# Attention beside a gated-Strassen feed-forward layer: first products taken apart, x reloads put back, `wo` in the q and k buffers

## The chip, the cores and the metric

The kernel runs on one core of a Trainium2 chip. The metric is device time in microseconds (us). Of the kernel before, three runs took 1152.2, 1151.22 and 1151.04 us; the median is 1151.22 us. The engines are TensorE (PE, with PEld for its weight loads), VectorE (DVE), ScalarE (ACT), GpSimd (POOL) and SyncE (SP); an engine executes its own queue in order and waits on semaphores for others. SP and POOL issue nearly all DMAs here.

## What is computed

x has 2048 rows of 576 numbers, all in fp32. It is normalised, and two branches of the result are added to x:

```python
def _A_ref(x, wqkv, wo):            # 32 heads of 18
    q, k, v = split(x @ wqkv)
    idx = pos[:, None] - arange(8) * 2          # 8 keys, every second position back
    logits = einsum("bhsd,bhswd->bhsw", q, k[idx]) * scale   # masked where idx < 0
    return einsum("bhsw,bhswd->bhsd", softmax(logits), v[idx]) @ wo

def _B_ref(x, w1, w2):              # 576 -> 4608 -> 576
    return maximum(x @ w1, 0) @ w2

xn = _layernorm(x)
return x + _A_ref(xn, wqkv, wo) + _B_ref(xn, w1, w2)
```

## The kernel before

The rows are taken in two phases (`ph`) of 1024 rows, each held as eight tiles `X[i]` of 128 rows. In a phase the 4608 columns of w1 come in 18 blocks `n` of 256; m = 18 ph + n counts them. Each block has two halves of 512 rows, and g = 2m + h numbers these 72 steps. Every fp32 product is made of parts: a number is cast to a high and a low part (`hi_lo`, L287: ACT makes the high part, DVE the low one), and PE multiplies high by high, high by low and low by high.

The products with w1 are made from step 4 on by a scheme of seven products instead of eight (`pstep`, L627: P1, P5, P6, P2, P7, P3, P4). It needs sums and differences of x (`xs`, forms S1 to S4, from `s_forms`, L379) and of w1 (a set of eight slots, `wset`, from `set_make`, L446: DMAs from a copy kept in DRAM, four DVE differences in `ts`, four casts of 512). Its results go through the PSUM banks `bk` and `bkA` and the SBUF sums `sn` to `hhi` and `hlo`. Between these steps the outputs of the step before are made: `o_step` (L743) multiplies h with w2 into `po`. `po` is seeded with x by ACT (`po<-x`) and copied back to x (`x<-po`). In the last block of a phase the row is stored (L783), and in phase 0 POOL then reloads it with the raw x of phase 1 (L785), for the seeds of phase 1.

Attention goes in four units `u` of eight heads per phase. Block `QP[ph][u]` projects q, k and v (`qkv_tile`, L802) into `qo`, `kk` and `v`; `halo` (L840) copies the seven neighbouring positions over by DMA (L843). Then DVE does the attention (L848): products and sums for the logits (L870, L873), softmax, products with v (L902), and eight transposes into a `pr` buffer (L916), which four DMAs write to DRAM in turned order (L923). There are two `pr` buffers. At block `WOP[ph][u]` `wo_make` (L541) loads the rows of wo and casts them; `wo_h` (L689) loads the turned output (`olo<-turned`, L704 and L708) and casts it to `ohi` and `olo`; `o_step` adds their products into `po`. u = 4 there stands for the 16 left-over columns per unit.

Near the end of phase 0, the second phase's x is prepared: `x_load` (L1035) fetches a tile into a `pr` buffer, `x_norm` (L1040) normalises it (the power for `rstd` is a POOL instruction, L321; the last step on DVE is L335), `x_raw` and `x_rest` (L1043, L1051) transpose it on PE through the bank `pm`, and ACT copies it to `kk`, `v` and `qo`, which are free for it at that time; `x_parts` and `x_done` make the parts.

The order of every queue is written out in advance by a planner (class `Order`, L54). A dictionary `plan` gives functions to (step, tick) places; one tick passes after each of the seven P products and each `o_step`. `send` and `keep` issue a DMA at that point on SP or POOL. `act` and `dve` put an operation with a due time into a list, and `pick` (L81) gives out, among the operations that are ready by the planner's clock, the one that is due first:

```python
                if best is None or op.due < best[0].due:
                    best = (op, now)
```

`later` puts attention's DVE work into a queue that is served when nothing else is ready. When a PE product or a DMA needs an operation that is not out yet, `force` gives it out first. All that is planned time; on the chip only the queues' order and the semaphores remain.

## Time and profile before

| | us |
|---|---|
| median of three runs | 1151.22 |
| the profiled execution | 1153.78 |
| its span, first to last instruction | 1152.0 |
| PE busy | 1126.6 |
| DVE busy | 822.0 |
| ACT busy | 754.0 |
| POOL busy | 201.3 |

The profile comes from one execution, and all its times count from the start of its span. Busy time is the time in which an engine worked on instructions; the registers' and DMA-issuing instructions are not in it. A wait is put down to the instruction whose semaphore came last. The granted clock (PEclk) is TensorE's clock as a share of full speed. DMA issues stand under SPq and POOL. In rows of instructions the columns are start, duration, engine, line, operation, output and inputs, the count, and in brackets the idle time ahead of it with what ended it.

### The profile page before, as it was taken

The page shows a single profiled execution, that of the slowest core. Times are in us where ns is not written, and L with a number is a line of the kernel's source. Part 1 is how long each engine was busy: PE and PEld are TensorE (multiplying, and loading weights), DVE is VectorE, ACT ScalarE, POOL GpSimd, SP SyncE. Part 2 cuts the span into 40 slices and gives each one's busy share as a digit, 9 for nine tenths or more (in the row PEclk, how much of TensorE's full clock was granted, in tenths as well). Part 3 has the DMA queues.
Part 4 walks back from the last instruction along what each step waited for, and adds up shares of the span by engine and source line. Part 5 has one row for each costly group of instructions (what it writes and reads, how often), then busy time and mean ns, then how long its engine had stood idle before and what let it go on. Part 6 is the DMA issues. An engine that isn't in the chain of part 4 may idle for free.

```text
span 1152.0 us, 22365 instructions
## 1 busy us (share of the span) xinstructions
PE 1126.6 (98%) x8528; PEld 1111.0 (96%) x8528; DVE 822.0 (71%) x1533; ACT 754.0 (65%) x1658; POOL 201.3 (17%) x408
## 2 busy tenths in 40 slices
PE   7999999999999999999989999999999999999998
PEld 6899999999999999999989999999999999999998
DVE  7649979872999179964783398688936995399831
ACT  5558457754777477676686577387737765577764
POOL 2323322531436122620120001000000000000000
PEclk9999999999999999999999999999999999999999
DMA  5254263553444344264362222231323222322322
GB/s 164 62 172 137 77 172 97 160 133 103 137 142 130 72 136 122 70 145 149 96 182 65 82 60 65 46 103 53 94 46 94 68 56 62 98 59 58 82 70 92
DMA packets 137788, 115.64 MB, mean 100 GB/s; under 512 B 56288, under 2 KB 115936, under 8 KB 136400
## 3 DMA queue, kind: packets, MB, share of 16 engines
q1 hardware_dynamic: 128192, 85.00, 26.8%
q0 software_dynamic: 9344, 28.91, 8.8%
q8 instruction: 67, 1.10, 0.4%
q14 instruction: 41, 0.34, 0.1%
q10 hardware_dynamic: 144, 0.29, 0.1%
HBM read 96.01 MB, written 36.50 MB: 115 GB/s over the span
## 4 chain that ended last, share of the span: by engine, by line
PE 87%; DVE 4%; DMA 3%; ACT 3%; issue 1%; SPq 1%; POOL 0%; ACTq 0%; DVEq 0%; POOLq 0%
PE po L285 40%; PE bk L285 27%; PE pm L285 15%; PE bkA L285 6%; DMA x<-in_x 1%; DVE wset L282 1%; ACT po L279 1%; ACT x L279 1%; ACT wset L279 1%; DMA turned<-pr 1%; DMA wset<-wqc 0%; DVE hlo L577 0%; DMA qo<-in_w 0%; SPq L551 0%; DVE ts L282 0%
## 5 line engine op out<-in xcount | busy, mean ns | idle before, releaser
L285 PE MATMUL po<-w2t,hhi 128*128 128x256 f32 (+1 forms) x2304 | 396.6, 294 | 2.1 <-ACT po L279 2.0
L285 PEld LDWEIGHTS po<-w2t,hhi 128*128 128x128 f32 x2304 | 335.1, 188 | 4.1 <-ACT po L279 3.1
L279 ACT ACTIVATE x<-po 128x576 f32<-128x576 f32 x286 | 186.2, 651 | 177.3 <-PE po L285 173.9
L285 PE MATMUL po<-w2t,hlo 128*128 128x256 f32 (+1 forms) x1152 | 244.3, 293 | 0.4 <-DVE hlo L577 0.4
L285 PE MATMUL bk<-xs,wset 128*128 128x256 f32 x1632 | 231.9, 278 | 2.1 <-DVE hlo L577 2.0
L285 PEld LDWEIGHTS bk<-xs,wset 128*128 128x128 f32 x1632 | 211.4, 188 | 3.5 <-DVE hlo L577 2.9
L285 PEld LDWEIGHTS po<-w2t,hlo 128*128 128x128 f32 x1152 | 190.3, 188 | 0.7 <-DVE hlo L577 0.7
L279 ACT ACTIVATE po<-x 128x576 f32<-128x576 f32 x286 | 186.9, 654 | 5.9 <-DVE x L282 0.2
L285 PE MATMUL pm<-wset,xa 128*128 128x432 f32 x768 | 171.4, 360 | 0.8 <-DVE wset L282 0.4
L285 PEld LDWEIGHTS pm<-wset,xa 128*128 128x128 f32 x768 | 140.4, 188 | 7.8 <-ACT qo L279 1.0
L285 PE MATMUL bk<-xa,wset 128*128 128x256 f32 x924 | 132.2, 281 | 4.0 <-DVE sn L282 2.4
L282 DVE TENSOR_TENSOR sn<-bk,sn 128x256 f32<-128x256 f32 x136 | 57.2, 421 | 103.7 <-PE bk L285 63.8
L411 POOL COPY spare<-hhi 1x1 f32<-1x1 f32 x176 | 78.1, 444 | 291.4 <-ACT hhi L279 291.4
L285 PEld LDWEIGHTS bk<-xa,wset 128*128 128x128 f32 x924 | 120.7, 191 | 4.8 <-DVE sn L282 2.8
L279 ACT ACTIVATE kk<-pm 128x144 f32<-128x144 f32 (+1 forms) x68 | 21.0, 308 | 120.2 <-PE pm L285 118.5
L282 DVE TENSOR_TENSOR w2t<-w2t 128x576 fp32r<-128x576 f32 (+1 forms) x72 | 54.1, 751 | 60.8 <-ACT w2t L279 60.2
L870 DVE TENSOR_TENSOR pr<-qo,kk 128x1152 f32<-128x1152 f32 x64 | 84.9, 1351 | 5.6 <-DMA turned<-pr 5.6
L902 DVE TENSOR_TENSOR pr<-lg,v 128x1152 f32<-128x1152 f32 x64 | 85.2, 1356 | 0.0
L873 DVE TENSOR_REDUCE lg<-pr 128x64 f32<-128x1152 f32 x64 | 83.7, 1345 | 0.0
L285 PE MATMUL bk<-xr,wset 128*128 128x256 f32 x426 | 83.5, 278 | 0.0
L279 ACT ACTIVATE hhi<-sn 128x256 fp32r<-128x256 f32 x136 | 56.0, 413 | 35.1 <-DVE sn L282 33.9
L282 DVE TENSOR_TENSOR wset<-wset 128x512 fp32r<-128x512 f32 (+2 forms) x120 | 71.7, 599 | 8.9 <-ACT wset L279 8.5
(133 smaller groups left out, 1484.8 us busy)
## 6 DMA issues: line engine op xcount, KB each, us to landing
w2t<-w2c SPq DMA_DIRECT2D x70, 288.0 KB, 3.0
wset<-w1c SPq DMA_DIRECT2D x106, 128.0 KB, 2.6
w1c<-in_w POOLq DMA_DIRECT2D x72, 144.0 KB, 2.7
w2c<-in_w POOLq DMA_DIRECT2D x72, 144.0 KB, 3.1
wset<-wqc SPq DMA_DIRECT2D x28, 216.0 KB, 2.6
out<-x SPq DMA_DIRECT2D x16, 288.0 KB, 2.1
wset<-w1c SPq DMA_DIRECT2D x70, 64.0 KB, 2.3
ts<-w1c SPq DMA_DIRECT2D x34, 128.0 KB, 2.8
```

Of the source, the lines that this page charges most:

```text
L279: nc.scalar.activation(o, i, func)
L282: nc.vector.tensor_tensor(o, a, b, op=op)
L285: nc.tensor.matmul(o, l, r, start=start, stop=stop, skip_group_check=True)
L411: nc.gpsimd.tensor_copy(spare[0:1], f32(LATEST[-1])[0:1, 0:1])
L870: nc.vector.tensor_tensor(pr[i], q, window(k, i), op=ALU.mult)
L873: nc.vector.tensor_reduce(s["lg"][:, i], pr.pop(i).rearrange(heads, d=Dh), axis=AX.X, op=ALU.add)
L902: nc.vector.tensor_tensor(pr[i].rearrange(heads, d=Dh), e, window(v, i).rearrange(heads, d=Dh), op=ALU.mult)
```

## The change

- Attention's products: the first two products for the logits and their sums ran as product, product, sum, sum. Now the first goes with its sum, then the second; for the planner the first waits for the halo alone and the second for the DMAs of the preceding unit's turned output (`OUT_`).
- Phase 1's raw x: the reload is not issued with the store of the row but four ticks later (`reloads`, `x_again`).
- `wo`: its rows for u = 0 to 3 go to the buffer of q of that unit (`qop`, now two pools of one buffer), not to a `v` buffer; the load waits for that unit's turned output. u = 0 moves one block earlier in both phases (`WOP`). A `v` buffer is given out only when its last readers are (`v_turn`).
- Due times: casts of sets 9 to 12 us instead of 6 to 9, of w2 12 instead of 7, of wo 10 instead of 8; the casts of S3 and S1 4.0 instead of 2.4, those of S2 and S4 9.0 instead of 4.0. P5, P6 and P3 wait each for the form that they read.
- Turned output: for the left-over, the load for the second half's first rows goes out at tick 21 of its step instead of tick 0 of the next. The last but one step's second load goes to a `pr` buffer (`SPARE`) at tick 5 of the last step.
- The set of block 19 is made at tick 6 of step 36, `x_rest` of the last tile moves from tick 13 to 14, `x_done` of the second half from tick 0 to tick 2.

The names `qo`, `rr` and `RD` point to buffers that are now taken from the pools at their use.

```diff
--- before.py
+++ after.py
@@ -26,7 +26,7 @@
 QP = ((0, 3, 7, 11), (1, 4, 8, 12))
-WOP = ((6, 9, 13, 16), (7, 10, 14, 17))
+WOP = ((5, 9, 13, 16), (6, 10, 14, 17))
 HALO = ((0, 112), (112, 127))
@@ -208,6 +208,7 @@
     w2p = pool("w2p", 4)
+    qop = [pool(f"qop{b}", 1) for b in range(2)]
     pad2 = pool("pad2", 1).tile([P, PADS[2]], F32, name="pad2")
...
@@ -249,7 +249,15 @@
-    def v_tile():
+    VLAST = [[], []]
+
+    def v_turn(last):
+
+        o_.force(VLAST.pop(0))
+        VLAST.append(last)
+
+    def v_tile(last=None):
+        v_turn([] if last is None else last)
         return vp.tile([P, 2176], F32, name="v")[:, 0 : (W - 1 + NI) * UD].rearrange("p (w c) -> p w c", w=W - 1 + NI)
@@ -265,8 +273,10 @@
     KR = [raw_view(KK), raw_view(KK)]
-    rr = [z.rearrange("p i c -> p (i c)")[:, 0 : 2 * TBN].rearrange("p (j c) -> p j c", j=2) for z in QO]
-    RD = [rr[0][:, 0], rr[1][:, 0]]
+    QO, rr, RD = [None, None], [None, None], [None, None]
+
+    def q_raw(b):
+        return qop[b].tile([P, NI * UD], F32, name=f"qo{b}")
@@ -385,13 +395,13 @@
         ok = []
-        for j, sl in ((1, 2.4), (0, 4.0)):
+        for j, sl in ((1, 4.0), (0, 9.0)):
             k = act(lambda j=j: copy(XS[h][:, 0, 2 * j : 2 * j + 2], KR[h][j]), 1024, [a4], slack + sl)
         ok += [r, dve(lambda: sub(XR[h][DR:P, 2], RD[h][0:DR], f32(XR[h][0:DR, 2])), TBN, [r], slack + 3.5)]
-        XOK[h, "s"] = ok
+        XOK[h, 10 + S1], XOK[h, 10 + S2], XOK[h, 10 + S4] = ok[0:2], ok[2:4], ok[4:6]
         return ok
@@ -500,10 +510,10 @@
         else:
-            parts(T1, T3, 4, TS[:, 0:2], [c1, c3], 6)
-            parts(T2, T4, 4, TS[:, 2:4], [c2, c4], 7)
-            parts(B11, B21, 2, z[:, B11 : B21 + 1 : 2], [got[B11], got[B21], c1, c4], 8)
-            parts(B22, RR, 2, z[:, B22 : RR + 1 : 2], [got[B22], got[RR], c2, c3], 9)
+            parts(T1, T3, 4, TS[:, 0:2], [c1, c3], 9)
+            parts(T2, T4, 4, TS[:, 2:4], [c2, c4], 10)
+            parts(B11, B21, 2, z[:, B11 : B21 + 1 : 2], [got[B11], got[B21], c1, c4], 11)
+            parts(B22, RR, 2, z[:, B22 : RR + 1 : 2], [got[B22], got[RR], c2, c3], 12)
         ts_free[0] = [*ok[T1], *ok[T3], *ok[T2], *ok[T4]]
@@ -513,7 +523,7 @@
         g = send(lambda: nc.sync.dma_start(f32(w[:, 1]), W2C[m % NP][f * P : (f + 1) * P]), 295, kept["w2", m % NP], 4.0)
-        W2OK[m, f] = hi_lo(w[:, 0], w[:, 1], f32(w[:, 1]), D, [g], 7 + 2 * f)
+        W2OK[m, f] = hi_lo(w[:, 0], w[:, 1], f32(w[:, 1]), D, [g], 12 + 2 * f)
@@ -539,11 +549,15 @@
     def wo_make(ph, u):
-        WO[ph, u] = w = vp.tile([P, 2, D], F32R, name="v")
+        if u < NU:
+            WO[ph, u] = w = qop[u % 2].tile([P, 2, D], F32R, name=f"qo{u % 2}")
+        else:
+            v_turn([])
+            WO[ph, u] = w = vp.tile([P, 2, D], F32R, name="v")
         z = f32(w)[:, 1]
         if u < NU:
-            got.append(send(lambda: nc.sync.dma_start(z, WOC[u * UD : u * UD + P, :]), 295, kept["wo",], 3.0))
+            got.append(send(lambda: nc.sync.dma_start(z, WOC[u * UD : u * UD + P, :]), 295, [*kept["wo",], *turned[ph, u], *OFREE[u % 2]], 3.0))
         else:
@@ -551,7 +565,7 @@
                     ))
-        WOOK[ph, u] = hi_lo(w[:, 0], w[:, 1], z, D, got, 8)
+        WOOK[ph, u] = hi_lo(w[:, 0], w[:, 1], z, D, got, 10)
@@ -636,14 +650,14 @@
-            t = pe(f, T8, [*ok[T1], *ok[RR], *XOK[h, "s"], *XOK[h, 1], *BANK[n3]])
+            t = pe(f, T8, [*ok[T1], *ok[RR], *XOK[h, 10 + S1], *XOK[h, 1], *BANK[n3]])
             BANK[n3] = [act(lambda: copy(SN5, b3), TBN, [t, *SNF[5]], 3)]
         elif name == "P6":
-            t = pe(lambda: terms(b2, slot(m, T2), sform(h, S2), False), T6, [*ok[T2], *BANK[n2]])
+            t = pe(lambda: terms(b2, slot(m, T2), sform(h, S2), False), T6, [*ok[T2], *XOK[h, 10 + S2], *BANK[n2]])
             BANK[n2] = [act(lambda: copy(SN2, b2), TBN, [t, *SNF[2]], 1.4)]
@@ -663,7 +677,7 @@
-            t = pe(f, T8, [*ok[B22], *BANK[n3]])
+            t = pe(f, T8, [*ok[B22], *XOK[h, 10 + S4], *BANK[n3]])
             a = dve(lambda: sub(SN2, b3, SN2, ALU.add), TBN, [t], 0.8)
...
@@ -697,7 +712,13 @@
             ni = 2
-            hi, lo = whp.tile([P, TBN], F32R, name="ohi"), whp.tile([P, TBN], F32R, name="olo")
+            if g == NG - 2 and j == 1:
+                if u < NU:
+                    SPARE[:] = [prp.tile([P, W * UD], F32R, name="pr")]
+                z = SPARE[0][:, 32 + 512 * (u == NU) :]
+                hi, lo = z[:, 0:TBN], z[:, TBN : 2 * TBN]
+            else:
+                hi, lo = whp.tile([P, TBN], F32R, name="ohi"), whp.tile([P, TBN], F32R, name="olo")
             WOH[g, u, j] = hi, lo
@@ -738,6 +759,16 @@
     XLAST = [None] * NI
+    reloads = []
+
+    def x_again():
+
+        for z in reloads:
+            z[0] -= 1
+        while reloads and reloads[0][0] <= 0:
+            _, i, s = reloads.pop(0)
+            XLAST[i] = o_.keep(lambda: nc.gpsimd.dma_start(X[i], x_v[1, i]), 295, s.end)
+
     POF = [[], []]
@@ -778,11 +809,13 @@
             i2 = 4 * G[after[0]][2] + 2 * after[1] + k
+            assert ph == 0 or XLAST[i2] is not None
             POF[k] = [act(lambda: copy(whole(k), X[i2]), D, [e, XLAST[i2]], 2.2)]
             if ph + 1 < NPH:
-                XLAST[i] = o_.keep(lambda: nc.gpsimd.dma_start(X[i], x_v[ph + 1, i]), 295, s.end)
+                XLAST[i] = None
+                reloads.append([4, i, s])
@@ -795,7 +828,8 @@
-    HALOOK = {}
+    HALOOK, VDONE = {}, {}
+    OUT_ = []
     KFREE = [[]]
@@ -803,7 +837,8 @@
             o_.force(KFREE[0])
-            VV[u % 2] = v_tile()
+            QO[u % 2] = q_raw(u % 2).rearrange("p (i c) -> p i c", i=NI)
+            VV[u % 2] = v_tile(VDONE.setdefault((ph, u), []))
             nc.gpsimd.memset(KK[0:1, 0 : W - 1, :], 0.0)
@@ -932,7 +967,7 @@
             OFREE[u % 2] = [send(lambda: nc.sync.dma_start(O16[:, :, 16 * u : 16 * u + 16], qo[:, :, P:UD]), 65)]
-            turned[ph, u] = blocks(OT[u], s["tr"], 4)
+            turned[ph, u] = OUT_[:] = blocks(OT[u], s["tr"], 4)
             if u == NU - 1:
@@ -946,12 +981,13 @@
         add = o_.later
-        first = True
+        done = [[] for _ in range(NI)]
+        done[0], done[1] = halo, OUT_
         for i in range(0, NI, 2):
-            for f in (qk_mul, qk_sum):
-                for j in (i, i + 1):
-                    z = add(lambda f=f, j=j: f(j), big, halo if first else (), 1.3 if f is qk_sum and j == NI - 1 else 0.0)
-                    first = False
+            pairs = [(f, j) for f in (qk_mul, qk_sum) for j in (i, i + 1)]
+            for f, j in pairs if i else [pairs[0], pairs[2], pairs[1], pairs[3]]:
+                after = done[j] if f is qk_mul else ()
+                z = add(lambda f=f, j=j: f(j), big, after, 1.3 if f is qk_sum and j == NI - 1 else 0.0)
         KFREE[0] = [z]
@@ -961,10 +997,11 @@
             for j in (i, i + 1):
-                add(lambda j=j: av_mul(j), big)
+                z = add(lambda j=j: av_mul(j), big)
             for w in (4, 2, 1):
                     add(lambda j=j, w=w: av_add(j, w), w * UD)
+        VDONE[ph, u].append(z)
         for i in range(NI):
@@ -981,7 +1018,9 @@
         p = m - 1
-        if p % NP in QP[p // NP]:
+        if m == NP + 1:
+            at(g, 6, set_make, m)
+        elif p % NP in QP[p // NP]:
             at(g + 1, 0, set_early, m)
@@ -1024,11 +1063,11 @@
                     else:
-                        when = (gg + 1, 0), (gg + 1, 12)
+                        when = (gg, 21) if h else (gg + 1, 0), (gg + 1, 12)
                     if gg == NG - 1:
                     for j in range(len(when)):
-                        at(*when[j], wo_h, gg, z, j)
+                        at(*((gg + 1, 5) if (gg, j) == (NG - 2, 1) else when[j]), wo_h, gg, z, j)
@@ -1078,6 +1117,8 @@
         KR[h] = raw_view(v_tile() if h else KK)
+        rr[h] = q_raw(h)[:, 0 : 2 * TBN].rearrange("p (j c) -> p j c", j=2)
+        RD[h] = rr[h][:, 0]
@@ -1088,7 +1129,7 @@
             ((34, 13), (34, 15), (34, 19), (34, 20)), ((34, 20), (34, 22), (35, 1), (35, 2)),
-            ((35, 3), (35, 5), (35, 9), (35, 11)), ((35, 7), (35, 13)),
+            ((35, 3), (35, 5), (35, 9), (35, 11)), ((35, 7), (35, 14)),
         )
@@ -1098,7 +1139,7 @@
         at(g, 0, x_parts, h, 0)
-        at(g, 0, x_done, h)
+        at(g, 2 * h, x_done, h)
@@ -1110,6 +1151,7 @@
         idx_now[1] += 1
+        x_again()
...
@@ -1249,8 +1291,6 @@
                 o(q, cnt[name])
-        if g == 4:
-            RD[:] = [rr[0][:, 0], rr[1][:, 0]]
     o_.finish()
```

More of the change, by code (lines that the diff above doesn't have):

```diff
@@ L241, in tile_body @@
     VV = {}
-    QO = [keep.tile([P, NI, UD], F32, name=f"qo{b}") for b in range(2)]
     SN5 = keep.tile([P, TBN], F32, name="sn5")
@@ L684, in tile_body @@
     WOH, WOHOK = {}, {}
+    SPARE = []
     OT = dram.tile([NU, NI, P, P], F32, name="turned")
@@ L1134, in tile_body @@
     x_first(3)
-    ST2 = QO[0].rearrange("p i c -> p (i c)").rearrange("p (f d) -> p f d", f=2)
+    ST2 = q_raw(0).rearrange("p (f d) -> p f d", f=2)
     for f in range(2):
@@ L1149, in tile_body @@
     KR[1] = [
-        QO[1].rearrange("p i c -> p (i c)")[:, 0 : 4 * TBN].rearrange("p (s k c) -> p s k c", s=2, k=2),
+        q_raw(1)[:, 0 : 4 * TBN].rearrange("p (s k c) -> p s k c", s=2, k=2),
         TS.rearrange("p s k c -> p (s k c)").rearrange("p (s k c) -> p s k c", s=2, k=2),
```

## The prediction

> **What bounds the kernel.** I read the page's busy times first, then TensorE's (PE) busy time in stretches of the span, then the list of what PE waited for. The page:
>
> ```profile
> PE 1126.6 (98%) x8528; PEld 1111.0 (96%) x8528; DVE 822.0 (71%) x1533; ACT 754.0 (65%) x1658; POOL 201.3 (17%) x408
> ```
>
> PE is busy for 1126.6 of the span's 1152.0 us, and the changed program issues as many products of the same shapes. So the other engines count only where PE stops for them, and at most 25.4 us are there to win. These are the stretches in which it stops; the columns are the length, PE's busy time with its instructions, the granted clock, the DMA share and GB/s:
>
> ```profile
> core 0 of [0], span 1152.0 us
> core 0: us, PE busy (x), PEclk, DMA share, GB/s
> 171.00:184.00 13.00, 9.86 (x75) 1.00 0.43 124
> 184.00:248.00 64.00, 63.11 (x505) 1.00 0.47 136
> 529.00:566.00 37.00, 34.30 (x267) 1.00 0.34 107
> 581.00:588.00 7.00, 3.60 (x18) 0.76 0.37 109
> 584.00:586.00 2.00, 2.00 (x10) 0.50 0.36 139
> 600.00:608.00 8.00, 6.37 (x47) 1.00 0.76 260
> 608.00:1131.00 523.00, 523.00 (x3998) 1.00 0.26 70
> 1131.00:1137.00 6.00, 4.73 (x36) 1.00 0.13 49
> ```
>
> Length less busy time is PE's idle time: 3.14, 0.89, 2.70, 3.40, 1.63 and 1.27 us, together 13.03 us. From 608 to 1131 us it is nil, although the same loops run there. The rest of the 25.4 us lies before 66 us, where the order hardly changes, and behind the last product. The waits after 66 us, with their sum, number and longest:
>
> ```profile
> PE bk L285 <- DVE sn L282: 2.4, 2, 1.3
> PE pm L346 <- DVE pr L335: 2.1, 1, 2.1
> PE po L285 <- ACT po L279: 2.0, 3, 0.9
> PE bk L285 <- DVE hlo L577: 2.0, 4, 0.7
> PE po L285 <- DVE ohi L282: 1.4, 1, 1.4
> PE pm L1054 <- ACT v L279: 1.3, 1, 1.3
> PE po L285 <- ACT ohi L279: 1.3, 1, 1.3
> PE po L285 <- DVE hlo L577: 0.4, 1, 0.4
> ```
>
> These come to 12.9 us: single events of 0.2 to 2.1 us, each with a cause of its own. The question is which of them each edit takes away, and whether the new order makes others.
>
> **The change, part by part.** *First products taken apart (171 to 184 us, 3.14 us).* Attention 1's first two products ran on VectorE (DVE) like this:
>
> ```profile
> 161.32 1.35 DVE L870 TENSOR_TENSOR pr<-qo,kk 128x1152 f32<-128x1152 f32 x1
> 168.28 1.36 DVE L870 TENSOR_TENSOR pr<-qo,kk 128x1152 f32<-128x1152 f32 x1 [5.61 <-DMA turned<-pr]
> ```
>
> The second needs the `pr` buffer that holds attention 0's turned output until its four DMAs have landed. For 5.61 us DVE stands there, and the additions into `sn` behind it, for which PE waits 2.4 us, stand too. SyncE's queue (SP) shows why the DMAs were late:
>
> ```profile
> 154.71 1.46 SPq L843 DMA_DIRECT2D kk<-kk  x2
> 156.28 1.55 SPq L843 DMA_DIRECT2D v<-v  x2
> 157.93 0.88 SPq L934 DMA_DIRECT2D o<-qo  x1
> 158.91 4.13 SPq L923 DMA_DIRECT2D turned<-pr  x4
> ```
>
> In the changed order the last two rows go first and the halo (`kk`, `v`) behind them, and on DVE the first product follows two more pieces of the gated phase (the addition into `sn` and two `hlo`), with its sum and another addition before the second product. With the rows' issue times, starting at 154.71 us, `turned` is out by 159.8 and the `kk` halo by 161.2 us. The halo's landing has this range (minimum, median, maximum):
>
> ```profile
> DMA to landing us min/median/max: 3.3/4.6/6.6
> ```
>
> So the halo is there by 164.5 to 167.8 us. The addition ahead of the first product waits for this group of PE:
>
> ```profile
> 166.61 0.84 PE L285 MATMUL bk<-xs,wset 128*128 128x256 f32 x6
> ```
>
> It ends at 167.45 us, and with the addition and two `hlo` the first product's turn comes after 168 us, when its halo has landed. I take the whole 3.14 us as won; bounds 0 (the halo comes late instead) and 3.14.
>
> *`wo` in the q buffers, u=0 one pair of column blocks earlier (184 to 248 us, 0.89 us).* The products, their casts and one weight load of 288 KB move from n=6 to n=5, and from 7 to 6 in phase 1; count and size stay. The `wqc` loads for the next attention then have no `wo` beside them. The loads wait for attention's DMA too, but that has landed long before (above). I take 0.4 us; bounds -1.0 (a stall like the longest `hlo` wait, 0.7 us, more than once) and 0.89.
>
> The casts for `wo` are the tightest spot of the steady part. In block n=13:
>
> ```profile
> 451.63 0.42 DVE L282 TENSOR_TENSOR olo<-olo,ohi 128x256 fp32r<-128x256 f32 x1
> ```
> ```profile
> 452.56 0.69 PE L285 MATMUL po<-v,ohi 128*128 128x256 f32 x4
> ```
>
> The cast ends 0.51 us before PE asks. The changed order puts this cast and that of the weights ahead of the last of the four set casts, where they stood behind all four, so the margin grows at most of the eight places. At n=5 the cast of `olo` still follows three set casts while attention 1 runs; I charge 0.5 us for it, with 0 and 2.0 us (four `olo` at the margin just read) as ends.
>
> *Due times (529 to 566 us, 2.70 us).* Set casts get due times 3 us later, w2 5 us, `wo` 2 us. The planner always takes the earliest due among the ready operations, so copies in and out of `po` overtake them. That is aimed at the waits of `po` for ACT (2.0 us, three of them, two here and one at 602 us). The second item here is the 1.4 us wait for `ohi`; its load was queued behind a set's loads:
>
> ```profile
> 547.88 1.11 SPq L458 DMA_DIRECT2D wset<-w1c  x2
> 549.03 1.10 SPq L471 DMA_DIRECT2D wset<-w1c  x2
> 550.18 1.98 SPq L708 DMA_DIRECT2D olo<-turned  x2
> ```
>
> The last row is now issued at the end of the step before, ahead of the set's loads and of their wait for PE, at least 2.3 us sooner (550.18 against 547.88). What it passes is delayed by two issues (1.3 us for a set that is wanted 18 us later, below). I take 2.3 of 2.70 us; bounds 0.9 (half of the `ohi` wait and no more) and 2.7.
>
> *x loads behind other work (581 to 588 us, 3.40 us and the clock).* GpSimd's queue:
>
> ```profile
> 576.36 0.61 POOL L785 DMA_DIRECT2D x<-in_x  x1 [5.33 <-ACT v L279]
> 576.98 0.56 POOL L321 TENSOR_TENSOR rstd<-mv,mhalf 128x1 f32<-128x1 f32 x1
> 581.33 0.59 POOL L785 DMA_DIRECT2D x<-in_x  x1 [3.79 <-ACT v L279]
> 581.94 0.57 POOL L321 TENSOR_TENSOR rstd<-mv,mhalf 128x1 f32<-128x1 f32 x1
> ```
>
> Each reload of an x row waits until the old row has been written out, and a `rstd` sits behind it. DVE's last normalisation starts after the second `rstd`, which ends at 582.5 us, and PE's turning had waited 2.1 us when it was done, so PE arrived near 581 us; the `v` copies that follow cost the 1.3 us at L1054. In the changed order the seventh `rstd` is ahead of all reloads and the eighth behind the first reload only, which is free at 576.4 us; then it waits for its own statistics alone, and an estimate from the two holds (the seventh runs at once, the second reload's 3.79 us are gone) puts it 3 to 4 us sooner, ahead of PE. The remainder turnings also move behind P4. In the same place the clock fell to 0.50: 0.76 on average over 7 us is 1.7 us lost, part of it idle; I count 1.3. The reloads themselves go out four ticks later; their rows are wanted only when the next phase's outputs are seeded, a step of the loop later, which covers that (without the cover each would cost up to those four ticks). I take 3.2 + 1.3 = 4.5; bounds 1.3 (only the L1054 wait) and 5.1.
>
> The Trainium skill, TensorE: Matmul & The Clock Gate, Part 1, says that the array falls back to half rate after an idle window of about 3.4 us. The trace does not agree in size, since the pause here is 2.1 us and the row shows 0.50 behind it; by the rule the pause would not be the cause, the clock would stay as it is, and the sum would be 1.3 us smaller.
>
> *Second phase's set later, S forms split (600 to 608 us, 1.63 us).* The casts of block NP+1 leave the stretch in which the last forms of x are made (its loads go out six ticks later), and P5 waits for S1 only. I take 1.2; bounds 0 and 1.63.
>
> *Turned output of the last blocks (1131 to 1137 us, 1.27 us).* The last loads no longer wait for a rotating buffer but go into a free `pr` tile before the preceding `out` stores. I take 1.2; bounds 0 and 1.27.
>
> **The sum.** 3.14 + 0.4 - 0.5 + 2.3 + 4.5 + 1.2 + 1.2 = 12.2 us. The profiled execution took 1153.78 us for a span of 1152.0, so it would become 1141.6. It lies 2.6 us above the median of the three runs, 1151.22 us; on that scale the forecast is 1139.0 us.
>
> **The rivals.** *The halo is late instead.* It now queues behind `turned`. If it lands 3 us after its usual range, DVE stands from 168.6 to 171 us and PE stops about as before: 3.14 us are not won, 1142.1 us. For it speaks that both share SP; against it the 6.6 us maximum.
>
> The Trainium skill, DMA: Bandwidth & Descriptors, Queues, rings and completion order, states that a DMA's completion lands only after earlier writes of the same DMA engine. No row here isolates it; by it this rival's chance rises.
>
> *The phase change stays DVE bound.* If x's forms, not `rstd`, set the pace, PE arrives sooner and waits for `xs` instead: of 4.5 + 1.2 only 1.5 us remain, 1143.2 us. DVE (the third busy time here) is nearly full behind the gap, which speaks for it:
>
> ```profile
> 588.00:600.00 12.00, 11.97 (x99) 11.97 (x100) 10.41 (x21) 10.59 (x21) 1.61 (x3) 1.00 0.71 194
> ```
>
> The four set casts that leave (0.69 us each, a row below) speak against.
>
> *Later casts hurt everywhere.* This one ends slower. The mechanism is a run of four set casts that, with its due time 3 us later, falls in front of a copy that PE waits for, at 34 blocks. Its price is the mean `po` wait, 2.0/3 = 0.67 us: 23 us less the 12.2 gives 1162 us. It decides from 0.36 us a block. Against it:
>
> ```profile
> 528.89 0.69 DVE L282 TENSOR_TENSOR wset<-wset 128x512 fp32r<-128x512 f32 x1
> ```
> ```profile
> 547.68 0.73 PE L285 MATMUL bk<-xa,wset 128*128 128x256 f32 x5
> ```
>
> The set's last cast ends 18 us before the block's P1, so 3 us are there, and the due times give way to the copies, not the reverse.
>
> *The waits only move.* Every gap returns elsewhere: 1151 us.
>
> **How the numbers follow.** The likeliest case, all parts in their bounds near the values taken, has 0.68 and 1136 to 1142 us by itself. The halo rival 0.09, the phase change 0.09, waits that move 0.05, slower 0.09. The largest win is all 13.03 us and the whole 1.7 us of clock, 1136.5; I go a little lower, 1135.3, for the slower first matmuls after each pause that would vanish. The upper end, 1146.5, holds both partial rivals together. Measurement cannot tell less than 0.2% (2.3 us) from no change; faster by more is 0.86, within it 0.05, slower 0.09.
>
> **What would show it.** After: no DVE wait on `turned` and PE's idle time around 171 us gone; no `rstd` behind a waiting reload, clock 1.00 throughout the phase change; `olo` issued before the set at n=16; no wait at 1131 us; PE busy near 1126 us in a span near 1139 us. The prediction is wrong if a new PE wait above 1 us stands at n=5 (about 205 to 235 us), if the first product waits for `kk<-kk`, or if short `po` or `hlo` waits show in the stretch after 608 us.

## The result and the profile after

The changed kernel takes 1137.05 us (median of four runs, 1135.61 to 1137.25) against 1151.13 us before in the same comparison (1150.14 to 1152.2): a ratio of 0.9875, with a 95% interval of 0.9858 to 0.9892. The forecast was 1139.0 us in 1135.3 to 1146.5. The profiled execution took 1137.1 us for a span of 1135.3 us, where before it was 1153.78 us for 1152.0.

The page of the changed kernel, its busy times:

```profile
PE 1120.7 (99%) x8528; PEld 1108.8 (98%) x8528; DVE 825.2 (73%) x1533; ACT 753.3 (66%) x1658; POOL 196.2 (17%) x408
```

PE's idle time went from 25.4 to 14.6 us, and its busy time fell by 5.9 us, although it issues the same 8528 products. Its waits after 66 us, with sum, number and longest, are three instead of the eight kinds of before:

```profile
PE bk L295 <- DVE hlo L591: 1.2, 1, 1.2
PE po L295 <- ACT po L289: 0.3, 1, 0.3
PE bk L295 <- ACT sn L289: 0.2, 1, 0.2
```

PE in stretches (length, busy time with instructions, granted clock, DMA share, GB/s):

```profile
171.00:184.00 13.00, 13.00 (x109) 1.00 0.46 134
529.00:566.00 37.00, 37.00 (x302) 1.00 0.38 118
581.00:588.00 7.00, 6.84 (x56) 1.00 0.81 222
588.00:600.00 12.00, 10.81 (x88) 1.00 0.69 226
608.00:1110.00 502.00, 502.00 (x3837) 1.00 0.26 69
```

All the stretches that stopped are full but for 1.2 us at 590 us and 0.2 us ahead of it, and the clock of 0.50 in the phase change is gone. SP's queue at attention 1, then DVE's, then POOL's at the phase change:

```profile
157.20 3.07 SPq L958 DMA_DIRECT2D turned<-pr  x4
160.37 2.05 SPq L878 DMA_DIRECT2D kk<-kk  x2
```
```profile
170.34 1.35 DVE L905 TENSOR_TENSOR pr<-qo,kk 128x1152 f32<-128x1152 f32 x1
171.61 0.42 DVE L292 TENSOR_TENSOR sn<-bk,sn 128x256 f32<-128x256 f32 x1
...
173.53 1.35 DVE L905 TENSOR_TENSOR pr<-qo,kk 128x1152 f32<-128x1152 f32 x1
```
```profile
566.07 0.55 POOL L331 TENSOR_TENSOR rstd<-mv,mhalf 128x1 f32<-128x1 f32 x1 [3.98 <-DVE mv L328]
567.43 0.67 POOL L770 DMA_DIRECT2D x<-in_x  x1 [0.81 <-ACT v L289]
569.04 0.87 POOL L331 TENSOR_TENSOR rstd<-mv,mhalf 128x1 f32<-128x1 f32 x1 [0.94 <-DVE mv L328]
```

`turned` goes out ahead of the halo, neither product waits, and both `rstd` wait only for their statistics (`mv`), as the prediction said.

**Where the time came from.** The k-th product of PE is the same work at the borders used here, so its start in the kernel before less its start in another trace tells how far the other is ahead. The table gives what is won (+) or lost (-) in each stretch, in us, with the stretches counted on the kernel before's own time. The last column is the sum without the first 66 us: there the traces differ by up to 2.3 us, although all the kernels begin alike, so the first column is left out of what follows.

| kernel | to 66 | to 165 | to 184 | to 290 | to 529 | to 567 | to 590 | to 612 | to end | from 66 on |
|---|---|---|---|---|---|---|---|---|---|---|
| the changed kernel | -1.3 | -0.2 | +4.2 | +1.5 | +1.2 | +3.6 | +5.1 | +0.6 | +2.1 | 18.0 |
| e1 old products | -0.1 | -0.1 | +4.2 | +1.6 | +1.2 | +3.6 | +4.9 | +0.4 | +2.1 | 18.0 |
| e2 reload at once | -1.2 | -0.2 | +4.2 | +1.6 | +1.2 | +3.5 | +1.1 | +0.3 | +2.1 | 13.8 |
| e3 old due times | -1.3 | -0.4 | +4.2 | +1.0 | +0.8 | +2.9 | +4.4 | -1.3 | +1.5 | 13.1 |
| e4 old turned steps | 0.0 | -0.1 | +4.2 | +1.4 | +1.2 | +1.7 | +5.1 | +0.6 | +0.4 | 14.5 |
| e13 old due times and products | -2.2 | 0.0 | +1.5 | +1.0 | -0.9 | +2.7 | +4.4 | -1.3 | +0.8 | 8.2 |
| e5b wo in v | -1.4 | -0.1 | +4.2 | +1.3 | +1.2 | +3.7 | +5.1 | +0.6 | +2.1 | 18.0 |
| e5c no wo edits | -0.7 | -0.1 | +4.2 | -8.9 | +1.2 | +3.5 | +5.1 | +0.6 | +2.0 | 7.6 |
| e10 set early | -0.6 | -0.1 | +4.2 | +1.6 | +1.2 | +3.7 | +4.9 | -0.7 | +2.0 | 16.8 |
| before + new products (e14) | -0.1 | 0.0 | +4.2 | +1.0 | -5.5 | 0.0 | 0.0 | -0.2 | 0.0 | -0.5 |
| before + new due times (e6) | -2.3 | -0.2 | +4.2 | -8.0 | +1.2 | +1.6 | +1.2 | -1.2 | +0.4 | -0.8 |
| e15: e6, planner told of v | -2.2 | -0.2 | +4.2 | -7.6 | +1.2 | +1.7 | +1.1 | -0.8 | +0.3 | -0.1 |

The changed kernel's row tells where. The others tell why, and there the prediction's picture of separate stalls, each with its own edit, does not hold.

### The profile page after: what moved, and what is told of

It is laid out like the page before. It is cut to its first block, busy times and chain, and to the rows that moved or that the text cites. A ratio compares the mean times of both kernels' runs of the same rounds, so it can differ in the third digit from the quotient of the medians.

```text
span 1135.3 us, 22346 instructions
## 1 busy us (share of the span) xinstructions
PE 1120.7 (99%) x8528; PEld 1108.8 (98%) x8528; DVE 825.2 (73%) x1533; ACT 753.3 (66%) x1658; POOL 196.2 (17%) x408
## 4 chain that ended last, share of the span: by engine, by line
PE 96%; ACT 1%; DVE 1%; issue 1%; DMA 0%; POOL 0%; ACTq 0%; DVEq 0%
PE po L295 44%; PE bk L295 30%; PE pm L295 15%; PE bkA L295 6%; ACT x L289 0%; DMA x<-in_x 0%; PE pm L356 0%; DVE wset L292 0%; DVE bst L321 0%; ACT po L289 0%; DVE xa L292 0%; ACT xs L289 0%; ACT xa L289 0%; PE bk L356 0%; DVE x L292 0%
## 5 line engine op out<-in xcount | busy, mean ns | idle before, releaser
L421 POOL COPY spare<-hhi 1x1 f32<-1x1 f32 x176 | 71.6, 407 | 291.5 <-ACT hhi L289 291.5
L911 POOL TENSOR_SCALAR_AFFINE_SELECT lg<-lg 1x512 f32<-1x512 f32 x8 | 10.0, 1246 | 438.0 <-DVE lg L908 438.0
```

The source lines that it names most:

```text
L421: nc.gpsimd.tensor_copy(spare[0:1], f32(LATEST[-1])[0:1, 0:1])
L911: nc.gpsimd.affine_select(out=z, in_=z, pattern=[[1, NI], [1, W], [0, HG]], compare_op=ALU.is_ge, fill=-1e9 / scale, base=1 - W, channel_m ...
```

## The experiments

The theory at the start: the gain is a sum of separate stalls, each taken away by one edit. The rivals: the due times do nearly all; or edits cover for each other. In the table and in each experiment the time is a median of four runs, or of ten for e13, e14, e6 and e15. e13, e14, e6 and e5b ran on a chip where the kernel before scattered from 1150.48 to 1161.76 us. Run beside the experiments, the kernel before had medians of 1152.55 us (e1 to e4), 1153.42 us (those four) and 1152.43 us (the rest), 1.3 to 2.3 us above its 1151.13 us in the comparison above. So 2 us between a median here and 1137.05 us are no evidence by themselves, and the stretches are the better measure.

**The first products in their old order (e1).**

```diff
-            for f, j in pairs if i else [pairs[0], pairs[2], pairs[1], pairs[3]]:
+            for f, j in pairs:
-        done[0], done[1] = halo, OUT_
+        done[0] = halo
```

> The changed kernel with attention's first two products and sums in the old order, and without the dependence on the turned output. Separate stalls (my theory): the second product stands 3 to 6 us for the DMAs of turned again, PE's idle time in 171 to 184 us is 2.5 to 3.2 us again, and with the slower restarts the kernel takes 2.7 to 4.2 us more than the changed one (1139.7 to 1141.3 us). Rival, the stall goes because turned is now issued ahead of the halo and not because of the products: the wait is under 1.5 us and the time stays within 1 us of 1137.05. Rival, the due times do nearly all: within 1 us as well, but with the wait of 3 us still in DVE's row and PE not waiting for it.

Measured: 1136.72 us (1135.87 to 1137.72), and no stall. The edit I had credited with 3.14 us brings nothing in this place. DVE's queue in e1:

```profile
168.95 1.35 DVE L905 TENSOR_TENSOR pr<-qo,kk 128x1152 f32<-128x1152 f32 x1
170.22 0.42 DVE L292 TENSOR_TENSOR sn<-bk,sn 128x256 f32<-128x256 f32 x1
170.56 1.35 DVE L905 TENSOR_TENSOR pr<-qo,kk 128x1152 f32<-128x1152 f32 x1
```

The second product has no wait, because `turned` still goes out ahead of the halo. Something else moved that.

**The old due times (e3).**

```diff
-            parts(T1, T3, 4, TS[:, 0:2], [c1, c3], 9)
+            parts(T1, T3, 4, TS[:, 0:2], [c1, c3], 6)
...
-        W2OK[m, f] = hi_lo(w[:, 0], w[:, 1], f32(w[:, 1]), D, [g], 12 + 2 * f)
+        W2OK[m, f] = hi_lo(w[:, 0], w[:, 1], f32(w[:, 1]), D, [g], 7 + 2 * f)
...
-        WOOK[ph, u] = hi_lo(w[:, 0], w[:, 1], z, D, got, 10)
+        WOOK[ph, u] = hi_lo(w[:, 0], w[:, 1], z, D, got, 8)
```

> The changed kernel with the old due times of the set casts (6 to 9), w2 (7) and wo (8). My theory: PE's waits of po for ACT, 2.0 us in all, and short hlo waits return at 450 to 610 us, and the kernel takes 1 to 3.5 us more (1138 to 1140.6 us). Rival, the due times are what brought most of the whole gain, the order around all other places following from them: 8 us or more (over 1145 us). Rival, the later casts cost time elsewhere: the kernel takes less than 1136 us.

Measured: 1141.79 us (1140.63 to 1142.66), 4.7 us more: above my figure, well below the rival's. PE's two longest kinds of wait in e3:

```profile
PE bk L295 <- DVE hlo L591: 2.4, 2, 2.0
PE po L295 <- ACT po L289: 0.9, 1, 0.9
```

The `po` wait is back as expected; the larger part is an `hlo` wait of 2.0 us at 592 us, in the phase change, and the clock behind it (below). And SP's queue has the halo first again:

```profile
156.47 1.48 SPq L878 DMA_DIRECT2D kk<-kk  x2
...
160.67 4.31 SPq L958 DMA_DIRECT2D turned<-pr  x4
```

So it is the due times that put `turned` first: with the set casts due later, attention 0 is given out sooner. Yet 171 to 184 us stays full in e3, where a sum now stands between the two products. DVE's queue in e3, the first sum and the second product:

```profile
164.47 1.35 DVE L908 TENSOR_REDUCE lg<-pr 128x64 f32<-128x1152 f32 x1
165.86 1.36 DVE L905 TENSOR_TENSOR pr<-qo,kk 128x1152 f32<-128x1152 f32 x1
```

The second product starts 0.9 us after the last `turned` issue has ended (164.98 us), though these DMAs took 3.8 us or more from issue to landing here. So it does not wait for them. The sum has freed the `pr` buffer of the first product, and in the built programs of e3 and e14 the second product has that address, where in the kernel before and in e13 it has the one that `turned` still reads. Either edit should be enough, each in its own way: the due times send `turned` off sooner, and the new order of products does without its buffer.

**Both undone (e13).** The diffs of e1 and e3 together.

> The changed kernel with both the old due times and the old order of attention's first products. Either edit undone by itself left 171 to 184 us without a stall: with the old products, turned was still issued ahead of the halo; with the old due times, the halo was first again but a sum stood between the products. Theory (two covers, each enough): here both are gone, the second product waits 4 to 6 us for turned, PE stops for 2.5 to 3.2 us in that stretch, and the kernel takes 3 to 4.5 us more than with the old due times alone (1141.8 us), so 1144.8 to 1146.3. Rival (a third edit, the wo casts or the v buffers, took the stall away): within 1 us of 1141.8.

Measured: 1148.82 us (1144.04 to 1151.47; span of the profile 1146.0). The stall is back; DVE in e13:

```profile
163.53 1.35 DVE L905 TENSOR_TENSOR pr<-qo,kk 128x1152 f32<-128x1152 f32 x1
168.99 1.36 DVE L905 TENSOR_TENSOR pr<-qo,kk 128x1152 f32<-128x1152 f32 x1 [4.12 <-DMA turned<-pr]
```

PE's idle time there is 1.9 us, less than I expected; the stretch wins 1.5 instead of 4.2 us. That confirms the two covers. The median is above the range I gave, and 1.7 us of it lie between 290 and 529 us, which I did not foresee.

**Each alone on the kernel before (e14, e6).** e14 puts only the new order of products and the dependence on `turned` into the kernel before (the lines of e1's diff, the other way round); e6 only the new due times (those of e3's diff, likewise).

> The kernel before with the new order of the first products and the dependence on turned, and nothing else. Theory: the stall at 171 to 184 us goes as it did with the old due times, PE is idle less than 0.7 us there, and the kernel is 2.5 to 4.5 us faster than before; all other waits (po 2.0, ohi 1.4, pr 2.1, v 1.3, ohi 1.3) stay. Rival (without the other edits the stall stays): same time as before within 1 us.

> The kernel before with the new due times of the set casts, w2 and wo, and nothing else. Theory: the due times alone put turned ahead of the halo, so the stall at 171 to 184 us goes too (3 to 4.2 us), and with it the po waits and the slow stretch at 450 to 483 us (2 to 3 us): 5 to 7.5 us faster than before; ohi at n=16, the rstd and L1054 waits at the phase change and the 1.3 us at the end stay. Rival (due times do nearly all): 10 us or more faster. Rival (they bring only the po waits): 1 to 3 us.

Measured: e14 1153.59 us (1148.25 to 1158.88; ratio 0.9992, interval 0.9962 to 1.0021), e6 1154.7 us (1154.01 to 1156.96; ratio 0.9995, interval 0.9971 to 1.0019). Neither is faster, and both expectations failed, though in both traces the stall at 171 to 184 us is gone with its full 4.2 us. In the profiled executions new stalls take it back. In e6, PE's wait, ACT's row and DVE's last products with v:

```profile
PE pm L285 <- ACT qo L279: 6.3, 1, 6.3
```
```profile
252.90 0.29 ACT L279 ACTIVATE v<-pm 128x144 f32<-128x144 f32 x1 [7.09 <-DVE pr L902]
```
```profile
250.25 2.62 DVE L902 TENSOR_TENSOR pr<-lg,v 128x1152 f32<-128x1152 f32 x2
```

Unit 2's first copy into `v` waits until attention 1 has made its last product with `v`: the two share a buffer. In the kernel before that wait was there too, and hidden, with nothing to spare:

```profile
249.25 0.29 ACT L279 ACTIVATE v<-pm 128x144 f32<-128x144 f32 x1 [0.45 <-DVE pr L902]
```

What used up that margin shows when PE's last products for the first tile of unit 2 are set beside DVE's last product with `v`. In the kernel before:

```profile
247.91 0.56 PE L285 MATMUL pm<-wset,xr 128*128 128x432 f32 x2
```
```profile
247.86 1.36 DVE L902 TENSOR_TENSOR pr<-lg,v 128x1152 f32<-128x1152 f32 x1
```

DVE ends 1.3 us behind that start of PE. In e6 PE starts there at 244.93 us and DVE ends at 252.87, 7.9 us behind. In e14, where PE has won the same 4.2 us, it is 1.0 us (242.78 and 243.74 us), and the copy follows at once, at 243.78 us. So PE's earlier arrival did not make this stall; the new due times did, which put DVE's products some 6.6 us later against PE. Which operations came ahead of them was not traced.

In e14 it is another place, at 358 us. The longest wait of 355 to 365 us, and ACT's row:

```profile
ACT hhi L279 <- POOL spare L411: 4.0, 1, 4.0
```
```profile
362.09 0.38 ACT L279 ACTIVATE hhi<-bkA 128x256 fp32r<-128x256 f32 x1 [3.96 <-POOL spare L411]
```

POOL reads one value of `hhi` (L411) ahead of each DMA that keeps weights, and ACT may not write that buffer before it has. Four such copies in a row, from 338.26 us on, show 2.64 to 7.62 us each there; the kernel before has one of 4.89 us at 358.32 us, and PE does not stop. Why POOL was late was not tested. e14's ten runs lie between 1148.25 and 1158.88 us, and one execution was profiled, so it stays open whether this stall belongs to the edit or to that execution.

**The wo part undone (e5b, e5c).** e5b only puts wo's weights back into the `v` buffers, at the new blocks. e5c undoes the whole part:

```diff
-WOP = ((5, 9, 13, 16), (6, 10, 14, 17))
+WOP = ((6, 9, 13, 16), (7, 10, 14, 17))
...
-        o_.force(VLAST.pop(0))
-        VLAST.append(last)
+        pass
...
-        if u < NU:
-            WO[ph, u] = w = qop[u % 2].tile([P, 2, D], F32R, name=f"qo{u % 2}")
-        else:
-            v_turn([])
-            WO[ph, u] = w = vp.tile([P, 2, D], F32R, name="v")
+        v_turn([])
+        WO[ph, u] = w = vp.tile([P, 2, D], F32R, name="v")
```

> The changed kernel with wo's weights in the v buffers as before, at the new blocks. Theory (the q buffers themselves bring little, the earlier block and the due times bring what was won at 184 to 285 us): within 1 us of 1137.05. Rival (the v buffers make v's next user wait): DVE or PE stands 1 us or more where v is asked for again, and the kernel takes 1 to 3 us more.

> The changed kernel with the whole wo part undone: weights in the v buffers, their products at the old blocks, and the planner not told when attention is done with a v buffer; everything else as changed. Theory (the wo part is a cover for the others): the next unit's v lies in the buffer that attention 1 still reads, as in the kernel before and in the one with the due times alone, so ACT's first v copy waits for DVE's last product with v, PE stops for 1.5 to 6.4 us near 247 us, and the kernel takes 1.5 to 7 us more than 1137.05. Rival (my prediction's reading: the wo part by itself is worth 0.4 less 0.5 us): within 1 us of 1137.05, no wait of pm for ACT above 0.5 us near 247 us.

Measured: e5b 1136.03 us (1135.73 to 1137.33), no change. e5c 1146.78 us (1145.79 to 1147.11): 9.7 us more, beyond even the 7 us at the end of what I expected. In e5c:

```profile
PE pm L294 <- ACT qo L288: 6.6, 1, 6.6
```
```profile
253.31 0.29 ACT L288 ACTIVATE v<-pm 128x144 f32<-128x144 f32 x1 [7.32 <-DVE pr L933]
```

The stall of e6 is here with everything else changed. The stretch to 290 us loses 8.9 us instead of winning 1.5. In the built programs unit 2's `v` has the address of attention 1's in the kernel before, e6, e15 and e5c; in the changed kernel and in e5b it has the other. There ACT copies while DVE is still at its last two products, which in e5b begin at 246.95 us and take 2.61:

```profile
247.88 0.28 ACT L289 ACTIVATE v<-pm 128x144 f32<-128x144 f32 x1
```

The wo part also brings DVE's products forward again: in e5c the last one ends 8.7 us behind the start of PE that was used above, in the changed kernel and in e5b 2.5 us. Even then a shared buffer would hold ACT's copy up, which goes at 247.71 us in the changed kernel while DVE works until 249.38. So the worth of the wo part is what it lets the other edits win. By itself, on the kernel before, it was not run. wo in the q buffers at the old blocks was not tried either; that the queues would then wait for each other is my guess.

**Telling the planner only (e15).** e6 with the changed kernel's `v_turn`: the planner gives out attention's last product with `v` before the buffer is taken again.

```diff
+    def v_turn(last):
+        o_.force(VLAST.pop(0))
+        VLAST.append(last)
...
+        VDONE[ph, u].append(z)
```

> The kernel before with the new due times, and the planner told when attention is done with a v buffer (the next unit's copies come behind the last product in its order); wo stays in the v buffers at the old blocks, so the buffer itself is shared as before. Theory (the 6.3 us wait of the kernel with due times alone came from DVE doing other work while the copy waited, which the planner could not see): DVE's products are hurried, the wait near 247 us falls from 6.3 to under 2.5 us, and the kernel is 4 to 8 us faster than before. Rival (the shared buffer alone sets the wait): it stays at 5 us or more and the kernel is as slow as before within 2 us.

Measured: 1154.53 us (1153.44 to 1156.05; ratio 1.0017, interval 1.0002 to 1.0032). The wait is 5.8 instead of 6.3 us:

```profile
PE pm L292 <- ACT qo L286: 5.8, 1, 5.8
```

My theory fell, and the rival's wait stands; the time, 2.1 us above the 1152.43 us of the kernel before beside it, is at the edge of the rival's 2 us. DVE's last product still ends 7.4 us behind the start of PE, where e6 had 7.9, so telling the planner hardly hurries it, and the shared buffer makes ACT wait for it. By what is left, the earlier block of `wo`, alone or with `v_turn`, brings DVE forward and v elsewhere; whether it would do without `v_turn` stays open.

**The reload at once (e2).**

```diff
-                XLAST[i] = None
-                reloads.append([4, i, s])
+                XLAST[i] = o_.keep(lambda: nc.gpsimd.dma_start(X[i], x_v[ph + 1, i]), 295, s.end)
```

> The changed kernel with each reload of x issued in the step of its store, not four ticks later. My theory (the rstd behind a waiting reload is the cause at the phase change): one or two rstd stand behind a reload for 3 to 5 us again, PE waits about 2 us between 566 and 592 us, the granted clock falls to 0.50 for about 2 us, and the kernel takes 2.0 to 4.6 us more (1139.0 to 1141.7 us). Rival, DVE's load set the pace there and the moved turnings and set casts brought the gain: rstd is late but PE's idle time grows by less than 0.5 us and the time stays within 0.7 us of 1137.05.

Measured: 1140.53 us (1139.12 to 1141.22), 3.5 us more; in the stretch to 590 us, 4.0. POOL's queue in e2, and PE in stretches:

```profile
567.27 0.61 POOL L817 DMA_DIRECT2D x<-in_x  x1 [5.38 <-ACT v L289]
567.89 0.57 POOL L331 TENSOR_TENSOR rstd<-mv,mhalf 128x1 f32<-128x1 f32 x1
572.23 0.59 POOL L817 DMA_DIRECT2D x<-in_x  x1 [3.76 <-ACT v L289]
572.84 0.57 POOL L331 TENSOR_TENSOR rstd<-mv,mhalf 128x1 f32<-128x1 f32 x1
```
```profile
572.00:574.00 2.00, 0.13 (x2) 1.00 0.22 39
574.00:576.00 2.00, 1.82 (x11) 0.74 0.66 256
576.00:578.00 2.00, 2.00 (x11) 0.50 0.00 0
```

This is the picture of the kernel before, pause and clock included. The delay of four ticks is the cause; the rival (DVE's load) is out.

**The turned output at the old steps (e4).**

```diff
-                        when = (gg, 21) if h else (gg + 1, 0), (gg + 1, 12)
+                        when = (gg + 1, 0), (gg + 1, 12)
...
-                        at(*((gg + 1, 5) if (gg, j) == (NG - 2, 1) else when[j]), wo_h, gg, z, j)
+                        at(*when[j], wo_h, gg, z, j)
...
-            if g == NG - 2 and j == 1:
+            if False:
```

> The changed kernel with the turned output's pieces loaded and split at the old steps (the second piece at tick 0 of the next step, and the last ones in rotating buffers). My theory: PE's wait for ohi at n=16 in phase 1 returns with 1.4 us near 550 us, and 1.3 us at 1131 to 1137 us, so the kernel takes 2.4 to 3 us more (1139.4 to 1140.1 us). Rival, the due times alone removed the wait at n=16: only the 1.3 us at the end return, 1138.3 us. Rival, both go anyway: 1137.0 us within 0.5.

Measured: 1139.7 us (1139.28 to 1140.8), with both waits back to the tenth:

```profile
PE po L295 <- DVE ohi L292: 1.4, 1, 1.4
PE po L295 <- ACT ohi L289: 1.3, 1, 1.3
```

They cost 1.9 us in the stretch to 567 us and 1.6 at the end, 0.5 and 0.3 more than their idle time. The due times alone do not remove the first.

**The second phase's set at the old tick (e10), and the last wait (e9).** First e10's edit, then the core of e9's, which casts the last forms of x in pieces of 512 instead of 1024.

```diff
-        if m == NP + 1:
-            at(g, 6, set_make, m)
-        elif p % NP in QP[p // NP]:
+        if p % NP in QP[p // NP]:
```
```diff
-            k = act(lambda j=j: copy(XS[h][:, 0, 2 * j : 2 * j + 2], KR[h][j]), 1024, [a4], slack + sl)
+            for y in (1, 0):
+                k = act(lambda j=j, y=y: copy(XS[h][:, 0, 2 * j + y], KR[h][j][:, y]), 512, [a4], slack + sl)
```

> The changed kernel with the set of block NP+1 made at the old step, six ticks earlier, in the stretch where the last forms of x are made. Theory: its loads and casts compete with the forms again, PE is idle 0.8 to 1.6 us more in 581 to 608 us and the kernel takes 0.8 to 2 us more than 1137.05. Rival (the split of the S forms, so that P5 waits for one form only, is what brought the gain there): within 0.5 us.

> The changed kernel with the last two forms of x cast in halves of 512 elements, not in one piece of 1024, so that ACT's and DVE's pieces for PE can go between them. Theory: the wait of 1.2 us for hlo at 590 us, the one that is left, came from an xs copy of 1.99 us in ACT's queue ahead of hhi; with halves it falls below 0.5 us and the kernel takes 0.7 to 1.5 us less than 1137.05. Rival (DVE's or ACT's load is what sets it, four more instructions make it worse): 1.2 us or more stay, time not less than 1137.

Measured: e10 1138.56 us (1137.63 to 1139.07), with waits of 1.7 us for `hlo` and 0.3 us for `xs` where the changed kernel has one of 1.2. The set's late tick is worth 1.2 us by the last column, 1.3 in the stretch to 612 us alone. e9 1137.32 us (1136.6 to 1138.28), and its wait is 1.1 us. ACT's rows in e9 tell why:

```profile
589.43 1.66 ACT L289 ACTIVATE xs<-v 128x512 fp32r<-128x512 f32 x3
590.99 0.36 ACT L289 ACTIVATE hhi<-bk 128x256 fp32r<-128x256 f32 x1
```

The planner puts three of the four halves ahead of `hhi`, so 1.66 us stand there instead of 1.99. On DVE three low halves (1.89 us) stand ahead of `hlo`, which starts 0.5 us after `hhi` is done. That the forms delay `hhi`, and with it PE, is only argued; e9 didn't shift them far enough to show it. No variant beats the changed kernel by more than their runs scatter.

## Why the prediction was right, step by step

**The total** was right and the sum short. Terms of 12.2 us stand against 16.7 between the two profiles and 18.0 from 66 us on; between the medians it is 14.1. That the forecast came within 2 us is in part luck: the profile of before lay 2.6 us above its median and that of after at its own. PE's busy time fell to 1120.7 us, where the prediction left it near 1126. None of its signs of being wrong came: no wait at n=5, none of the first product for `kk<-kk`, no short ones after 608 us.

**First products (3.14 us, measured 4.2).** The stretch was right, the cause half right: taking the products apart wins nothing while the due times put `turned` first. I had put the new order of SP down to this edit, but it belongs to the due times. What the edit does by itself I had not seen: the second product no longer needs the buffer of `turned` (e3). The size was short because a pause costs more than its idle time. In the kernel before, the group behind a pause and one in full flow:

```profile
172.55 0.97 PE L285 MATMUL bk<-xa,wset 128*128 128x256 f32 x6 [1.07 <-DVE sn L282]
...
181.53 0.85 PE L285 MATMUL bkA<-xa,wset 128*128 128x256 f32 x6
```

That is 0.12 us. In all, each pause costs 0.3 to 0.5 us more than it shows: (4.2 - 3.1) / 3 here for three waits, 1.6 - 1.3 for one at the end of the kernel, 1.9 - 1.4 for the one that e4 brings back at 548 us. Where the rest beyond the 0.12 us goes is not shown; an overlap of products that is lost around the pause is my guess.

**wo in the q buffers (0.4 less 0.5, measured +1.5 in its stretch; 10.4 us are lost there without it).** This is the step that failed. I counted its own stalls and charged 0.5 us for casts, and did not ask what the other edits would run into without it. The clue was a row I did not quote: ACT's copy at 249.25 us with 0.45 us of wait on attention's products. The due times put these products 6.6 us later against PE (e6), and only the wo part makes up for that. Neither that loss nor its cover stood in the sum, and since the edits came together the two cancel: on this point the total came out right by luck. (`wo` goes to the two buffers of q; that of k, which the title names, has no part in it.)

**Due times (2.3 us with the `ohi` load, measured 3.6).** Right in cause: the `olo` load goes out at 540.22 us, ahead of the set's loads at 541.50. e4 gives 1.9 of it to the earlier `olo`, and e3 0.7 to the due times; the rest goes with either. Missed: what the due times do elsewhere, 4.9 us in all by the last column (18.0 less 13.1), above all at the phase change. Another 1.0 us of the changed kernel's gain lies between 445 and 500 us, where four products of the kernel before took 0.69 to 0.70 instead of 0.68 us; e6 has the same 1.2 us in the column to 529 us, so the due times bring it, but that slow stretch itself is unexplained.

**x loads (4.5 us, measured 5.1).** Right: both `rstd` early, PE not waiting, clock at 1.00. e2 puts 4.0 of it on the reloads alone, pause and clock together.

**The second phase's set (1.2 us, measured 0.6).** The term's size was right: undone alone (e10) the stretch to 612 us loses 1.3 us. But 0.7 us of that make up for a loss that the rest of the change brings there (-0.7 in e10), which I had not counted; and 1.2 us of idle time stay at 590 us. This is the rival that the phase change stays bound by the forms, in a small part; it was priced at 1143.2 us and did not come to that.

**Last turned output (1.2 us, measured 1.6).** Right, with the pause's 0.3 us.

**The rivals.** The halo was not late: the first product waits for nothing. Later casts did not hurt in the changed kernel: with the old due times it is slower. Alone on the kernel before they did hurt, but in one place, by attention's products (e6), not at 34 blocks. The waits did move in e6, and in the profile of e14, where single edits were tried; that rival had the right mechanism, for a change that leaves a part out. The rule of the Trainium skill, TensorE: Matmul & The Clock Gate, Part 1, in the reading by which a pause of 2.1 us would not lower the clock, was not borne out: in e2 pause and clock return together.

## What to carry to other kernels

Before crediting an edit with a stall, look for waits with a few tenths of margin in the queues of the engines that are off the critical path (here one ACT row with 0.45 us), and ask which of their releasers the edit moves: due times that were changed for copies and casts moved attention's products by 6.6 us. A product that waits for a buffer can be helped by sending the buffer's reader off sooner or by not needing that buffer, and the rows of the two queues tell which of them happened. In a kernel whose order is planned, one part can be worth more for what it lets the others win than for its own stalls; test a part by taking it out of the whole as well as by putting it in alone. And in this kernel count 0.3 to 0.5 us more than its idle time for each short pause of PE, and a stretch of half clock for one of 2 us or more.

## What the runs showed of the hardware

The granted clock depends on the length of a pause, and not at once. A wait of 1.5 us (e15) and one of 1.7 us (e10) left it at 1.00; those of 2.0 to 6.6 us were each followed by 0.50. PE in stretches: the end of the 1.7 us pause in e10, then the pause of 2.0 us in e3, then that of 6.4 us in e6.

```profile
589.30:591.00 1.70, 0.02 (x1) 1.00 0.98 340
591.00:594.00 3.00, 2.69 (x20) 1.00 0.69 212
```
```profile
592.00:594.00 2.00, 0.06 (x1) 1.00 0.97 365
594.00:595.50 1.50, 1.50 (x13) 0.99 0.53 137
595.50:598.50 3.00, 3.00 (x15) 0.50 0.72 258
```
```profile
247.00:253.40 6.40, 0.08 (x1) 0.90 0.00 0
253.40:258.40 5.00, 4.97 (x14) 0.50 0.24 66
```

In e3 the clock falls 1.5 us after PE has gone on working, and stays low for 3 us; in e6 it is low from the first product and for 5 us; in e5c, behind 6.6 us, for 3 us. In the traces' own records of the clock the stretches at 0.50 are 3.41 us long behind pauses of 2.0 to 2.2 us and 6.83 us behind the one of 2.3 us (e14) and those of 5.8 to 6.6 us, where they begin within the pause. The stretches at 1.00 between two falls are whole multiples of 3.413 us: 552.96 us in the kernel before, 162 of them. The fall in e3 comes at 595.46 us, and in the 3.41 us that end there PE was busy for 1.52 us. The Trainium skill, TensorE: Matmul & The Clock Gate, Part 1, tells of a window of about 3.4 us that runs freely, so that the moment of a change depends on where in it the work lies. The delay in e3 and the unequal lengths agree with that; a whole idle window isn't needed by these rows, as 2.0 us were enough.
